# Places of 256 rows for the loaded rows of a routed expert layer, with small blocks loaded further ahead

## The chip, the cores and the metric

The kernel runs on one core of a Trainium2 chip. The metric is the device time of one execution in microseconds, the median of three runs. The engines are TensorE (PE, with its weight loads PEld), VectorE (DVE), ScalarE (ACT), GpSimd (POOL) and SyncE (SP). SP computes nothing here. It issues DMAs, one after another in the order of its queue, and a DMA that has to wait holds up every DMA behind it.

## The reference

A causal convolution of seven taps over 8 x 3584 tokens of 192 numbers (eight heads, each with its own taps), then a mixture of eight experts in which each token goes to one expert.

```python
w = softmax(weight)                                     # 8 heads x 7 taps
x = conv(x, w).reshape(28672, 192)                      # causal, per head
xn, en = x / (norm(x) + 1e-6), emb / (norm(emb) + 1e-6)
logits = xn @ en.T / tau
expert_idx = argmax(logits); gate_w = softmax(logits)[expert_idx]
for e in range(8):                                      # hidden width 1024
    mask = expert_idx == e
    out[mask] = gate_w[mask] * (relu(x[mask] @ w1[e]) @ w2[e])
```

## The kernel before

**Two streams.** The 28672 tokens come in 16 chunks of 1792 tokens (c0 to c15). A chunk is loaded (`load_x`, L355), convolved on PE (`mix`, L381), scaled and split into half-precision rows (`scaled`, `rest`), and turned by DMA transposes from SBUF to SBUF into `xtb` (`turn`, L619: four groups g of four transposes a chunk, all issued on SP). PE makes the logits from `xtb` (`logits`, L607), DVE ranks the tokens by expert (`rank`, L513, from the reduction at L518 to the row numbers `di` at L578), and POOL scatters the rows into the DRAM tensor `rows_d`, sorted by expert, in 16 indirect DMAs a chunk (`put` and `scatter`, L627). This is the dispatch stream.

The expert stream works off blocks of rows of one expert. `fetch` (L736) loads one block into SBUF: a register load, two DMA transposes from `rows_d` into the tile `e_xT` (L750) and one small DMA of token numbers and gates (L754), all on SP. `expert` (L772) makes the hidden layer, 40 matmuls into `h_ps` for a block of up to 256 rows and as many of 512 columns for one of 512 (L796), and then 24 matmuls into `o_ps` for each 128 rows (L819). Results are scaled by ACT (L824) and scattered to the output by POOL (L826).

**Blocks.** `hand_out` cuts blocks whenever enough chunks are ranked: b0 to b6 (256 rows) need the scatters of c0 and c1, b7 to b13 (256) those up to c2, b14 to b16 (512) and b17 to b24 (256) those up to c4, b25 to b31 (512) and b32 to b38 (256) those up to c7, b39 to b48 (512) those up to c11. The last 43, of 512, 256 and 128 rows mixed, need all (`last_blocks`). In all there are 37 loads of 256 rows, 34 of 512 and 21 of 128. `subs` holds the blocks in order, with the number of scatters that each needs. The index `at` is the block being worked on, `ready` the next to be loaded.

**What sets the order.** `run` (L930) interleaves the two streams by a plan of costs: after each step of a block it takes steps of the dispatch stream that are due, and one `put`. The order of SP's queue is that of the program (`manual_schedule`). On the other engines a scheduler orders the instructions when the kernel is built, by priority in the program and by what it thinks is ready; `behind` (L118) only keeps a convolution or logits matmul from going ahead of its planned place.

**Loading ahead.** `expert` calls `fetch` until the blocks up to `at + 2` are loaded. `e_xT` is a ring of three buffers of 512 rows, whatever the block's size, so a load waits until the block three before it has been through its `h_ps` matmuls. A load also waits for the scatters it needs. Two of the ring's buffers serve in the head of the kernel for other things: `head` (identity and ones for the norms of the weights, L173 and L315) and `cseq` (L225).

Of the kernel before, what the change touches and what calls it, by code (L numbers as in the profile page):

```python
# [12 lines left out]
F16 = mybir.dt.float16  # L13
F32 = mybir.dt.float32
# [8 lines left out]
H = 8  # L23
# [37 lines left out]
LEAD = 16.0  # L61
CAP = 6.0
MARGIN = 22
AHEAD_STEPS = 36


# [8 lines left out]
class _Moe:  # L75
    def __init__(self, ctx, tc, x, weight, emb, tau, w1, w2, out):
        self.tc, self.nc = tc, tc.nc
        self.x, self.weight, self.emb, self.tau = x, weight, emb, tau
        self.w1, self.w2, self.out = w1, w2, out
        B, S, _ = x.shape  # L80
        self.B, self.S, self.N = B, S, B * S
        self.nch = self.N // CT
        self.per_b = S // CT
        self.cap = self.N + PAD
        self.dummy = E * self.cap
        pool = lambda name, bufs, **k: ctx.enter_context(
            tc.tile_pool(name=name, bufs=bufs, **k))
        self.cp = pool("const", 1)
        self.xp = pool("xload", 2)
        self.sp = pool("small", 2)  # L90
        self.lp = pool("lone", 1)
        self.ep = pool("expert", 3)
        self.yp = pool("y", 3)
        self.op = pool("out", 4)
        self.mp = pool("meta", 6)
        self.rings = {k: pool("ps_" + k, n, space=PSUM)
                      for k, n in (("r", 2), ("l", 1), ("h", 5))}

        self.res = self.cp.tile([128, E * RES], F16, name="res")
        self.work = self.cp.tile([128, 2 * NFC * 512 + S2 + RES - W2], F16, name="work")  # L100
        self.hid = self.work[:, 0:2 * NFC * 512]
        self.slot = self.work[:, 2 * NFC * 512:]
        self.xtb = self.cp.tile([128, NT // GX, XW + HALO], F16, name="xtb")
        self.rows2 = self.cp.tile([TP, 2, NT, RW], I32, name="rows2")
        self.ids = self.cp.tile([TP, NT], I32, name="ids")
        self.xtn = 0
        self.wexp = self.cp.tile([128, E, 2], I32, name="wexp")
        self.dp = pool("scratch", 1, space=DRAM)
        self.rows_d = self.dp.tile([E * self.cap + PAD, RW], I32, name="rows_d")
        self.scatters, self.pend, self.step = [], [], None  # L110
        self.nput, self.final = 0, False
        self.counts, self.pace = {}, 1.0
        self.xts, self.mixed = [], {}
        self.subs, self.ready, self.at, self.copied = [], 0, 0, 0
        self.clock, self.mm = 0.0, None
# [51 lines left out]
    def constants(self):  # L167
        nc, cp = self.nc, self.cp
        nc.gpsimd.memset(self.xtb[:, :, XW:], 0.0)
        nc.gpsimd.memset(self.rows2[:, :, :, XD + 2:], 0)  # L170
        nc.gpsimd.iota(self.ids, pattern=[[TP, NT]], base=TP - 1,
                       channel_multiplier=-1)
        head = self.ep.tile([128, 4 * 512], F16, tag="xT", name="head")[:].bitcast(F32)  # L173
        self.idf, self.onef = head[:, 0:128], head[:, 128:256]
        make_identity(nc, self.idf)
        self.idh = cp.tile([128, 128], F16, name="idh")
        nc.vector.tensor_copy(out=self.idh, in_=self.idf)
        nc.gpsimd.memset(self.onef, 1.0)
        self.oneh = cp.tile([128, 128], F16, name="oneh")
        nc.gpsimd.memset(self.oneh, 1.0)  # L180

        self.lth = cp.tile([128, 128], F16, name="lth")
        nc.gpsimd.memset(self.lth, 1.0)
        nc.gpsimd.affine_select(
            out=self.lth, in_=self.lth, pattern=[[1, 128]], base=0,
            channel_multiplier=-1, compare_op=ALU.is_gt, fill=0.0)

        tmp = self.op.tile([128, D], F32, tag="y", name="tmp")[:, 0:2 * E + 64].bitcast(I32)
        e8i = tmp[0:TP, 0:E]
        nc.gpsimd.iota(e8i, pattern=[[-1, E]], base=E, channel_multiplier=0)  # L190
        self.e8 = cp.tile([TP, E], F32, name="e8")
        nc.vector.tensor_copy(out=self.e8, in_=e8i)

        self.rst = cp.tile([TP, E, NT], F32, name="rst")
        nc.gpsimd.memset(self.rst, 1.0)
        nc.gpsimd.memset(self.rst[:, :, 0:1], 0.0)

        nums = tmp[0:1, E:E + 64]
        nc.gpsimd.iota(nums, pattern=[[1, 64]], base=0, channel_multiplier=0)
        self.nums = cp.tile([1, 64], F32, name="nums")  # L200
        nc.vector.tensor_copy(out=self.nums, in_=nums)

        cbi = tmp[:, E + 64:]
        nc.gpsimd.iota(cbi, pattern=[[self.cap, E]], base=0, channel_multiplier=0)
        self.cb = cp.tile([128, E], F32, name="cb")
        nc.vector.tensor_copy(out=self.cb, in_=cbi)

        self.start = cp.tile([1, E], F32, name="start")
        nc.vector.tensor_copy(out=self.start, in_=cbi[0:1, :])

    def conv_taps(self, w):
        nc, cp = self.nc, self.cp
        m = cp.tile([H, 1], F32, name="cw_m")
        nc.vector.reduce_max(out=m, in_=w, axis=AX.X)
        nc.vector.tensor_scalar(out=w, in0=w, scalar1=m[:, 0:1], scalar2=None,
                                op0=ALU.subtract)
        z = cp.tile([H, 1], F32, name="cw_z")
        nc.scalar.activation(out=w, in_=w, func=AF.Exp)
        nc.vector.reduce_sum(out=z, in_=w, axis=AX.X)
        nc.vector.tensor_single_scalar(out=z, in_=z, scalar=1e-9, op=ALU.add)  # L220
        nc.vector.reciprocal(out=z, in_=z)
        nc.vector.tensor_scalar(out=w, in0=w, scalar1=z[:, 0:1], scalar2=None,
                                op0=ALU.mult)

        seq = self.ep.tile([128, 3 * 512], F16, tag="xT", name="cseq")[  # L225
            0:H, :].bitcast(F32)[:, 0:2 * 128]
        nc.vector.memset(seq, 0.0)
        nc.vector.tensor_copy(out=seq[:, TP + 9:TP + 9 + KT], in_=w)
        sd = self.dp.tile([H, 2 * 128], F32, name="cseq_d")
        nc.sync.dma_start(out=sd, in_=seq)  # L230
        self.more()
        self.band = cp.tile([128, H, TP], F32, name="band")
        run = sd[:, 0:TP]
        nc.sync.dma_start(out=self.band, in_=bass.AP(
            tensor=run.tensor, offset=run.offset,
            ap=[[1, 128], [2 * 128, H], [1, TP]]))
# [496 lines left out]
            out=self.slot[:, S2:], in_=self.res[:, bass.ds(self.we + W2, RES - W2)])  # L733


    def fetch(self):  # L736
        nc, tc = self.nc, self.tc
        sel, j, n, u, need = self.subs[self.ready]
        while len(self.scatters) < need:
            self.put()  # L740
        if u == 0:
            self.row = nc.sync.value_load(sel[0:1, j, 1:2], min_val=0,
                                          max_val=E * self.cap + PAD - n)
        row = self.row + u if u else self.row
        T = min(n, 512)
        nj = T // 128
        xT = self.ep.tile([128, 4 * 512], F16, tag="xT", name="e_xT")[
            :, 0:4 * T].rearrange("p (k t) -> p k t", t=T)
        src = self.rows_d[:].bitcast(F16)
        lds = [nc.sync.dma_start_transpose(  # L750
            out=xT[:, k:m], in_=src[bass.ds(row, T), o:o + 128 * (m - k)]).ins
            for k, m, o in ((0, 3, 0), (3, 4, 2 * D - 64))]
        mt = self.mp.tile([128, 4, 2], I32, tag="mt", name="e_mt")[:, 0:nj]
        lds.append(nc.sync.dma_start(  # L754
            out=mt, in_=self.rows_d[bass.ds(row, T), XD:XD + 2].rearrange(
                "(j p) c -> p j c", p=128)).ins)
        for i in lds:
            tc.declare_no_dep(i, group="put", keep=self.scatters[:need],
                              reason="loads name the scatters they need")
            tc.add_to_no_dep_group("get", i)  # L760
            for s in self.scatters[:need]:
                _dep(tc, i, s.name)
        self.subs[self.ready] = (sel, j, n, u, xT, mt, T)
        self.ready += 1
# [6 lines left out]

    def expert(self):  # L772
        nc, tc = self.nc, self.tc
        while self.ready < min(self.at + 3, len(self.subs)):
            self.fetch()
        sel, j, n, u, xT, mt, T = self.subs[self.at]
        self.copy_w1(self.at)
        if u == 0 and n >= 512:
# [116 lines left out]
    def steer(self, spent):  # L895
# [9 lines left out]
        self.rate = min(self.rate, 3.0)  # L905
        self.pace = (NT * self.end - self.nput) / max(1.0, steps - MARGIN)
        if self.final:
# [124 lines left out]
```

## Time and profile before

| | |
|---|---|
| time, median of 3 runs | 1249.96 us (1249.76 to 1250.8) |
| profiled execution, its own time | 1245.91 us |
| its span | 1244.2 us, mean granted TensorE clock 0.961 of full speed |
| PE busy | 1135.9 us, 91% of the span |
| DVE, ACT, POOL busy | 763.8, 592.5, 552.6 us |
| `h_ps` matmuls of small blocks (weights copied to `work`) | 2320, 232.4 us |
| loads of blocks | 184 transposes of `e_xT` in 92 loads |
| transposes of `xtb` by SP | 224 |

Times inside the execution are microseconds from the start of the span. A row of the engine timeline gives the start, the length, the engine, the line, the operation and how many were merged. Brackets at its end say how long the engine had been idle before it and what ended that. In the windows view PEclk is the granted clock of TensorE as a share of 2.4 GHz.

### The profile page before, as it was taken

The numbers are of one execution on the slowest core, as the hardware profiler recorded it, in microseconds if no ns is written. First come the engines' busy times: TensorE is split into PE (matmuls) and PEld (weight loads), VectorE is DVE, ScalarE is ACT, GpSimd is POOL, SyncE is SP. The second block draws the span as 40 slices with busy tenths as digits, with TensorE's granted clock in tenths as the row PEclk, the third lists the DMA queues.
The fourth block names the chain that finished last, engine by engine and source line by source line (L and its number), as shares of the span: only waits on it lengthen the run. The fifth ranks groups of instructions, "written<-read, shape, count | busy, mean of one in ns | idle before, by whom it ended". The sixth has DMA issues, their size and how long they took to land.

```text
span 1244.2 us, 31794 instructions
## 1 busy us (share of the span) xinstructions
PE 1135.9 (91%) x10620; PEld 881.2 (71%) x10620; DVE 763.8 (61%) x2042; ACT 592.5 (48%) x1359; POOL 552.6 (44%) x525
## 2 busy tenths in 40 slices
PE   4765869899999899998999999989999999999998
PEld 2543758776677876766887667757877786898797
DVE  3899667885766856666766474653335544465364
ACT  4986335455564464563546463333333434333333
POOL 0074166573565554646745456672222121222222
PEclk9676889999999999999999999999999999999999
DMA  9745576566666596654657645333222131223121
GB/s 255 216 146 147 120 162 147 119 168 145 135 157 165 97 185 146 131 140 97 165 105 170 115 94 125 87 96 66 65 45 61 41 75 43 43 54 72 42 52 28
DMA packets 305962, 140.69 MB, mean 113 GB/s; under 512 B 247774, under 2 KB 296285, under 8 KB 305808
## 3 DMA queue, kind: packets, MB, share of 16 engines
q1 hardware_dynamic: 282000, 87.97, 34.1%
q0 software_dynamic: 23808, 50.69, 14.7%
q8 instruction: 94, 1.54, 0.5%
q14 instruction: 60, 0.49, 0.1%
HBM read 38.35 MB, written 51.35 MB: 72 GB/s over the span
## 4 chain that ended last, share of the span: by engine, by line
issue 27%; PE 15%; POOL 8%; DMA 2%; ACT 1%; DVE 1%; POOLq 1%; ACTq 0%; DVEq 0%
POOL out_dram L826 7%; PE h_ps L796 7%; PE o_ps L819 6%; PE conv_ps L388 1%; DMA rows_d<-rows,di 1%; POOL rows_d L627 1%; DMA out_dram<-y,e_mt 1%; DMA xtb<-rows 0%; POOLq L826 0%; ACT work L800 0%; ACT sq L401 0%; PE lg_ps L611 0%; ACT rows L437 0%; DVE work L802 0%; DVE rows L444 0%
## 5 line engine op out<-in xcount | busy, mean ns | idle before, releaser
L819 PE MATMUL o_ps<-work 128*128 128x192 f16 x5544 | 503.2, 248 | 21.1 <-DVE work L802 9.2
L819 PEld LDWEIGHTS <-work 128*128 128x128 f16 x5544 | 462.5, 98 | 60.4 <-DVE work L802 15.7
L826 POOL DMA_INDIRECT out_dram<-y,e_mt x231 | 257.0, 1113 | 479.1 <-ACT y L824 439.2
L802 DVE SCALAR_TENSOR_TENSOR work<-h_ps,work 128x512 f16<-128x512 f32 x462 | 314.4, 685 | 175.2 <-ACT work L800 169.7
L800 ACT ACTIVATE work<-h_ps 128x512 f16<-128x512 f32 x462 | 271.3, 596 | 240.3 <-PE h_ps L796 206.1
L627 POOL DMA_INDIRECT rows_d<-rows,di x256 | 281.2, 1098 | 140.7 <-issue 57.1
L796 PE MATMUL h_ps<-e_xT,res 128*128 128x512 f16 x1360 | 311.2, 380 | 8.5 <-DVE work L802 5.9
L796 PEld LDWEIGHTS <-res 128*128 x1360 | 131.5, 98 | 162.7 <-issue 20.2
L796 PE MATMUL h_ps<-e_xT,work 128*128 128x256 f16 (+1 forms) x2320 | 232.4, 256 | 14.8 <-DMA e_xT<-rows_d 10.6
L796 PEld LDWEIGHTS <-work 128*128 128x128 f16 x2320 | 193.6, 99 | 40.7 <-DMA e_xT<-rows_d 9.9
L824 ACT ACTIVATE y<-o_ps,g 128x192 f32<-128x192 f32 x231 | 94.2, 419 | 235.6 <-PE o_ps L819 213.7
L732 DVE COPY work<-res 128x3074 f16 x88 | 85.3, 969 | 163.9 <-PE o_ps L819 163.8
L388 PE MATMUL conv_ps<-xt,band 128*112 128x384 f32 x256 | 112.5, 542 | 13.6 <-ACT xt L391 5.2
L437 ACT CAST rows<-xt 112x768 f16<-112x768 f32 x64 | 53.0, 832 | 97.4 <-DMA rows_d<-rows,di 49.2
L391 ACT COPY xt<-conv_ps 112x384 f32<-112x384 f32 x128 | 60.4, 480 | 43.0 <-PE conv_ps L388 41.5
L401 ACT ACTIVATE sq<-xt 112x192 bf16<-112x192 f32 x204 | 73.6, 361 | 4.8
L444 DVE TENSOR_TENSOR rows<-xt,rows 112x512 f16<-112x512 f32 x64 | 43.9, 685 | 45.7 <-ACT rows L437 35.3
L388 PEld LDWEIGHTS conv_ps<-xt,band 128*112 128x112 f32 x256 | 42.8, 194 | 32.0 <-issue 13.1
L435 DVE TENSOR_TENSOR xt<-xt,x_p_s 112x768 f32<-112x768 f32 x64 | 58.5, 950 | 0.0
L729 DVE COPY work<-res 128x3072 f16 x58 | 55.5, 957 | 0.3 <-PE h_ps L796 0.3
L611 PEld LDWEIGHTS <-xtb 128*128 128x128 f16 x768 | 30.1, 98 | 26.1 <-DMA xtb<-rows 12.9
L611 PE MATMUL lg_ps<-ma,xtb 128*128 128x16 f16 x512 | 30.6, 171 | 14.0 <-ACT xtb L502 7.1
(157 smaller groups left out, 520.5 us busy)
## 6 DMA issues: line engine op xcount, KB each, us to landing
xt<-in_dram SPq DMA_DIRECT2D x8, 1536.0 KB
xt<-in_dram SPq DMA_DIRECT2D x7, 1440.0 KB
rows_d<-rows,di POOLq DMA_INDIRECT x256
out_dram<-y,e_mt POOLq DMA_INDIRECT x231
xtb<-rows SPq DMA_TRANSPOSE x224
res<-in_dram SPq DMA_DIRECT2D x4, 768.0 KB
work<-in_dram SPq DMA_DIRECT2D x4, 768.0 KB
e_xT<-rows_d SPq DMA_TRANSPOSE x184
```

What stands on the lines that cost most here:

```text
L388: self.behind(nc.tensor.matmul(out=ps, lhsT=self.band[:, h, :], rhs=xt[:, :, h * G:(h + 1) * G], start=True, stop=True))
L391: nc.scalar.copy(out=xc[:, :, h * G:(h + 1) * G], in_=ps)
L401: nc.scalar.activation(out=sq, in_=xc[:, t, :], func=AF.Square, accum_out=n2[:, t:t + 1])
L611: i = self.nc.tensor.matmul(out=lg[:, g * GX + a, :], lhsT=xT[:, u:u + 128], rhs=self.mb if k == 2 else self.ma, start=(k == 0), stop=(k = ...
L627: i = self.nc.gpsimd.indirect_dma_start(out=self.rows_d[:, :], out_offset=bass.IndirectOffsetOnAxis(ap=idx, axis=0), in_=src, in_offset=No ...
L732: self.nc.vector.tensor_copy(out=self.slot[:, S2:], in_=self.res[:, bass.ds(self.we + W2, RES - W2)])
L796: mm = nc.tensor.matmul(out=ps[:, c, :], lhsT=w1(o, b + c), rhs=xT[:, k, :], start=(i == 0), stop=(i == 4))
L800: self.step = nc.scalar.activation(out=hh[:, b:b + m, :], in_=ps, func=AF.Relu).ins
L802: nc.vector.scalar_tensor_tensor(out=hl[:, b:b + m, :], in0=ps, scalar=0.0, in1=hh[:, b:b + m, :], op0=ALU.max, op1=ALU.subtract)
L819: mm = nc.tensor.matmul(out=o, lhsT=h[:, c, q], rhs=w2[:, c, k:k + D], start=(c + i == 0), stop=(c == NFC - 1 and i == 2))
L824: self.step = nc.scalar.activation(out=y, in_=o, func=AF.Copy, scale=g[:, a:a + 1]).ins
L826: i = nc.gpsimd.indirect_dma_start(out=self.out[:, :], out_offset=bass.IndirectOffsetOnAxis(ap=mt[:, a, 0:1], axis=0), in_=y, in_offset=No ...
```

## The change

The ring of three tiles becomes one tile `xr` of six places of 256 rows, the same memory. A block of up to 256 rows takes one place, one of 512 two neighbouring places that begin at an even one (`place`). `used` holds the last block in each place. `ahead` takes over from the loop in `expert`. Blocks up to `at + 2` are loaded as before. Beyond that a block is loaded as long as its places belong to blocks before `at` and its scatters have already been issued in the program. The head's helpers move into `xr`: `head` into places 0 and 1, `cseq` into place 2. The ring of the small tiles of token numbers goes from 6 to 10.

```diff
+HALF = 4 * 256
-        self.ep = pool("expert", 3)
-        self.mp = pool("meta", 6)
+        self.mp = pool("meta", 10)
+        self.xr = self.cp.tile([128, 6 * HALF], F16, name="xr")
+        self.turn_at, self.used = 0, [-1] * 6
-        head = self.ep.tile([128, 4 * 512], F16, tag="xT", name="head")[:].bitcast(F32)
+        head = self.xr[:, 0:2 * HALF].bitcast(F32)
-        seq = self.ep.tile([128, 3 * 512], F16, tag="xT", name="cseq")[
-            0:H, :].bitcast(F32)[:, 0:2 * 128]
+        seq = self.xr[0:H, 2 * HALF:].bitcast(F32)[:, 0:2 * 128]
+    def place(self):
+        w = 1 if self.subs[self.ready][2] <= 256 else 2
+        i = (self.turn_at + w - 1) // w * w % 6
+        return i, w
+
+    def ahead(self):
+        while self.ready < len(self.subs):
+            i, w = self.place()
+            near = self.ready < self.at + 3
+            if max(self.used[i:i + w]) >= self.at or not near and (
+                    self.subs[self.ready][4] > len(self.scatters)):
+                assert not near
+                return
+            self.fetch()
+
     def fetch(self):
         nc, tc = self.nc, self.tc
+        i, w = self.place()
+        self.turn_at = (i + w) % 6
+        self.used[i:i + w] = [self.ready] * w
...
-        xT = self.ep.tile([128, 4 * 512], F16, tag="xT", name="e_xT")[
-            :, 0:4 * T].rearrange("p (k t) -> p k t", t=T)
+        xT = self.xr[:, i * HALF:i * HALF + 4 * T].rearrange("p (k t) -> p k t", t=T)
...
     def expert(self):
         nc, tc = self.nc, self.tc
-        while self.ready < min(self.at + 3, len(self.subs)):
-            self.fetch()
+        self.ahead()
```

Worked through by hand from these rules and the order of the steps, the queue of SP reads as follows up to block 16. F3 is the load of b3, T3a and T3b are the two pairs of groups of transposes of chunk c3 (8 transposes each), X5 is the load of chunk c5, and a line is what stands between the starts of two blocks in the program.

```
        before                        after
start   F0 F1 F2 T2a X4 T2b           F0 F1 F2 T2a X4 T2b
b0                                    F3 F4 F5
b1      F3 T3a X5 T3b                 F6 T3a X5 T3b
b2      F4
b3      F5
b4      F6                            F7 F8 F9
b5      F7 T4a X6 T4b                 F10 T4a X6 T4b
b6      F8                            F11
b7      F9                            F12
b8      F10                           F13
b9      F11 T5a X7 T5b                T5a X7 T5b
b10     F12
b11     F13
b12     F14                           F14 F15
b13     F15 T6a                       T6a
b14     F16 X8 T6b                    F16 X8 T6b
b15     F17                           F17 F18
b16     F18 T7a X9 T7b                F19 F20 T7a X9 T7b
```

## Rows read from the trace of the kernel before

**Rows 1.** Busy time by stretch: PE, PEld, DVE, ACT, POOL, PEclk, DMA share, GB/s
```profile
290.00:850.00 560.00, 532.55 (x4723) 394.37 (x4722) 356.11 (x1067) 277.49 (x669) 322.17 (x302) 0.99 0.59 130
850.00:1100.00 250.00, 248.58 (x2384) 192.45 (x2383) 112.27 (x174) 95.22 (x179) 60.29 (x59) 1.00 0.25 53
```

**Rows 2.** Who waited for whom, PE, whole span: us in total, times, longest
```profile
PE lg_ps L611 <- DMA xtb<-rows: 11.8, 9, 3.6
...
PE h_ps L796 <- DMA e_xT<-rows_d: 10.6, 3, 6.0
```

**Rows 3.** Timeline of PE, 172 to 269 us: start, length, idle before and its end
```profile
172.92 0.21 PE L611 MATMUL lg_ps<-ma,xtb 128*128 128x16 f16 x2 [3.28 <-DMA xtb<-rows]
...
181.09 3.98 PE L796 MATMUL h_ps<-e_xT,work 128*128 128x256 f16 x22 [6.02 <-DMA e_xT<-rows_d]
184.90 0.20 PE L611 MATMUL lg_ps<-ma,xtb 128*128 128x16 f16 x2
...
227.19 1.27 PE L796 MATMUL h_ps<-e_xT,work 128*128 128x256 f16 x10 [3.66 <-DMA e_xT<-rows_d]
...
268.10 0.49 PE L796 MATMUL h_ps<-e_xT,work 128*128 128x256 f16 x3 [0.94 <-DMA e_xT<-rows_d]
```

**Rows 4.** Busy time by stretch around the two longest of these waits
```profile
174.00:184.00 10.00, 3.31 (x21) 2.31 (x21) 3.74 (x15) 1.99 (x3) 7.56 (x9) 0.50 0.75 142
...
228.00:232.00 4.00, 4.00 (x35) 3.01 (x32) 2.78 (x9) 1.19 (x2) 3.39 (x3) 0.57 0.54 119
```

**Rows 5.** Timeline of SP, 148 to 285 us: start, length of issuing, merged count
```profile
148.13 3.31 SPq L750 DMA_TRANSPOSE e_xT<-rows_d  x2
...
152.25 11.58 SPq L623 DMA_TRANSPOSE xtb<-rows  x8
...
164.54 12.34 SPq L623 DMA_TRANSPOSE xtb<-rows  x8
177.69 2.53 SPq L750 DMA_TRANSPOSE e_xT<-rows_d  x2
...
193.07 2.53 SPq L750 DMA_TRANSPOSE e_xT<-rows_d  x2
...
196.37 11.12 SPq L623 DMA_TRANSPOSE xtb<-rows  x8
...
208.67 13.37 SPq L623 DMA_TRANSPOSE xtb<-rows  x8
...
281.41 2.63 SPq L750 DMA_TRANSPOSE e_xT<-rows_d  x2
```

**Rows 6.** All loads of blocks: ns of one transpose, least/median/most, first and last start
```profile
L750 SPq DMA_TRANSPOSE e_xT<-rows_d x184: 1123/1232/2433, 111.1 to 1219.6; - x184
```

**Rows 7.** Timeline of PE, start of b14 (first matmuls with 512 columns)
```profile
289.50 0.81 PE L796 MATMUL h_ps<-e_xT,res 128*128 128x512 f16 x3
```

**Rows 8.** Timeline of DVE: first and last step of ranking chunks c3 and c4
```profile
185.91 0.41 DVE L518 TENSOR_REDUCE l<-lg_ps 112x128 f32<-112x256 f32 x1
...
201.92 0.17 DVE L578 TENSOR_SCALAR di<-dr 112x16 int32<-112x16 f32 x1
...
228.80 0.42 DVE L518 TENSOR_REDUCE l<-lg_ps 112x128 f32<-112x256 f32 x1
...
249.88 0.23 DVE L578 TENSOR_SCALAR di<-dr 112x16 int32<-112x16 f32 x1
```

**Rows 9.** Timeline of POOL: first and last of the 16 scatters of chunk c4
```profile
251.18 0.95 POOL L627 DMA_INDIRECT rows_d<-rows,di  x1 [0.30 <-DVE sl_ge L679]
...
278.20 1.24 POOL L627 DMA_INDIRECT rows_d<-rows,di  x1 [0.30 <-issue]
```

**Rows 10.** Timeline of PE: b0's matmuls and the first logits of chunk c2
```profile
116.84 4.53 PE L796 MATMUL h_ps<-e_xT,work 128*128 128x256 f16 x40
...
125.12 0.21 PE L611 MATMUL lg_ps<-ma,xtb 128*128 128x16 f16 x2 [3.59 <-DMA xtb<-rows]
```

**Rows 11.** Matmuls that read the head's ones: ns of one, first and last start
```profile
L315 PE MATMUL n_ps<-w_acc,head x16: 230/312/374, 22.6 to 104.1; 128*128 128x2 f32 x16
```

## The prediction

> **What bounds the kernel now.** I read the busy times by stretch first. From 290 us on PE is busy 532.6 of 560 us and then 248.6 of 250 us [rows 1], so whatever moves the time must either shorten PE's work, which this change does not touch, or take away idle time of PE before 290 us. The list of waits then says how much of that idle time is due to loaded rows: PE waited for `e_xT` three times, 10.6 us in all [rows 2]. The timeline shows all three: 6.02 us before b4, 3.66 us before b8 and 0.94 us before b12, and 3.28 us for transposes of chunk c3 just ahead of b4 [rows 3]. They add up to 13.9 us. Around them the granted clock is at its lower level of 1.2 GHz: 0.50 in the stretch 174 to 184, in which PE was busy 3.31 us, and 0.57 over 228 to 232 [rows 4]. At full clock that work would have taken 3.31 x 0.5 = 1.7 us and 4.00 x 0.43 = 1.7 us less. All that could be won is thus 13.9 + 3.4 = 17.3 us. The many small blocks after 850 us wait for no load at all (the three waits are the whole of it), so loading them earlier is worth nothing.
>
> Next is why these loads were late. SP's timeline shows the loads F4, F8 and F12 as the first behind the transposes of a chunk. For F4, a load takes its turn at 148.13 (F3), sixteen transposes and a load of x fill SP from 152.25 to 176.88, F4 starts at 177.69 [rows 5], and PE goes on at 181.09 [rows 3], 3.4 us after that start. SP, not the memory, was the queue that was full.
>
> **The change part by part.**
>
> *Number of instructions.* There are 92 loads before and after, with the same two transposes and one small DMA each, and the same 224 transposes of `xtb`. Nothing is added on any engine. What moves is the place of the loads in SP's queue. Blocks of 512 rows keep their distance of two.
>
> *Head.* `head` now lies in places 0 and 1, where F0 goes first, while before F0 had a free buffer. Its last reader starts at 104.1 [rows 11], and the first load at 111.1 [rows 6]. The wait is covered by 7 us. Without that cover it would be a delay of F0 by as much as the reader came later. The ring of 10 small tiles costs nothing in time, as nothing waits on it here.
>
> *Loads that move ahead of b4, b8 and b12.* F4, F5 and F6 now stand before T3a instead of behind T3b. F8, F9 and F10 stand before T4a, and F12 and F13 before T5a. The three waits for rows (10.6 us) and the clock's 3.4 us go.
>
> *What they are put in front of.* This is the other half. SP's queue is passed by three more loads before T3a and, in sum, three more before T4a (F0 to F10 instead of F0 to F7). One load takes 152.25 - 148.13 = 4.1 us of SP [rows 5]. So T3a and X5 start about 12.3 us later, at 164.6, and T3b ends at 189.2 instead of 176.9. F7 must wait for the scatters of c2 and cannot start before about 193.07, as now. Four loads follow, and T4a starts near 193.1 + 4 x 4.1 = 209.5 instead of 196.37: 13 us later. T4b ends at 208.67 + 13.37 + 13 = 235 instead of 222 [rows 5]. Before T5a the surplus is two loads, but one of those moves is already counted.
>
> What waits for T3 and T4: the logits on PE, the ranking on DVE, the scatters on POOL, and at last F14, the first load that needs c4. If PE meets the logits of c3 in the old place it idles (below). If it has b4 to b6 in SBUF it can do these first. Rows of the kernel before say that the order does give way: the logits of c2 are called before b0 in the program, and on PE the first of them stand behind all 40 `h_ps` matmuls of b0 and still wait 3.59 us for their transposes [rows 10]. I take it that this happens again, with new waits of 0 to 4 us at T3 and T4; 2 us.
>
> *The chain behind T4.* Now: T4b ends at 222, ranking runs from 228.80 to 249.88 (21.1 us) [rows 8], the scatters from 251.18 to 279.44 (28.3 us) [rows 9], F14 starts at 281.41 [rows 5], and b14 starts on PE at 289.50 [rows 7], 4.7 us after F14's data could be there (281.41 + 3.4). After: the logits of c4 can end about 1.3 us behind T4b, at 236.3. Ranking takes between 16.0 us (c3, 185.91 to 201.92) and 21.1 us (c4) [rows 8]. PE and DVE are then ahead of their plan, so the ranking's steps are the oldest work on DVE, and I take 16. The scatters take 28.3 us as now or, at the least, 16 times their spacing of 1.25 us = 20 us if POOL's scatters of results lie elsewhere (an estimate from lengths of 0.95 us and the 0.30 us before each [rows 9]); I take 25, nearer to the measured end. So 236.3 + 16 + 1.3 + 25 + 2 = 280.6 for F14, and 284.0 for its data. PE itself would be ready for b14 at 289.5 - 17.3 + 2 = 274.2. It therefore waits some 10 us there, in a new place, and comes back with the lower clock for a stretch (1.7 us, as after the wait at 181). b14's work then stands at 284.0 + 1.7 = 285.7, which is 3.8 us earlier than now. With the short ends (16, 20) F14's data is there at 279.0, a gain of 8.8; with the long ends (21.1, 28.3) at 292.4 and a loss of 4.6, each with the 1.7.
>
> *One rule against this.* Two transposes of a load take about 2.5 us of SP whether the block has 256 rows (177.69) or 512 (281.41) [rows 5], and the median of all 184, 128 rows among them, is 1.23 us each [rows 6]. The time is that of issuing. The Trainium skill, in DMA: Bandwidth & Descriptors, section Issuing engines are not separate DMA queues, says that the time a sequencer needs to initiate a DMA is usually small beside the DMA itself. By that, three more loads in front of T3 would hardly move it; the row says otherwise, since PE went on only 0.9 us after the issuing of F4 had ended.
>
> *After b14.* From there every load of the first 512 blocks waits as before, and later stages have no wait for rows to lose. What is won or lost at b14 stays to the end.
>
> **The rivals.**
>
> A. *The chain as long as now.* F14's data at 292.4 as worked out, b14 2.9 to 4.6 us late: the stall has only changed its place. For it: the scatters ran nearly back to back already [rows 9], and T4 had just 6 us to spare. Against it: PE's 17 us of freed time. The time is +3 us. It decides where ranking and scatters together take over 47 us.
>
> B. *PE's order stays as it is* (slower). Place: the logits of c3. T3b ends at 189.2, so the last group, which now starts at 184.90 [rows 3], starts at about 190, and PE idles at each group on the way. b4's wait is gone but PE is 5 us behind, with 1.7 us more at the lower clock. F14 comes no earlier than 284 there too, and the 3.66 us at b8 turn into a wait for T4b. The time is +6 us. It decides where the logits keep their place ahead of b4's matmuls.
>
> C. *SP is not held up.* If the transposes of T3 and T4 were as early as now, all of the 17.3 us less 2 would be won: -15 us. This is what the rule above gives. Against it stand the rows of issuing.
>
> D. *The change does not do what it says*: if the one tile `xr` were tracked as a whole, each block would wait for the load issued last, and behind every chunk's transposes (12 us and more a pair) PE would stand still. With some 10 us for each of the ten chunks from c3 to c12 that would be +100 us. Nothing in the trace speaks for it; the loads write separate column ranges.
>
> **How the numbers follow.** The profiled execution took 1245.91 us, 4.05 us under the median of 1249.96. Differences are carried over to the median. The forecast, -4 us, gives 1246.0, with its own range of 1240 to 1249; chance 0.46. A: 1253, chance 0.19. B: 1256, chance 0.18. C: 1235, chance 0.09. D: 1350, chance 0.02. The remaining 0.06 is for a new order on the engines that moves the time by 2 us either way. The range leaves out D, most of C and the far end of B: 1237 to 1256. A measurement of this kernel can tell about 0.2%, 2.5 us, from no change. The forecast case is faster by more than that in four of five outcomes, C always, so faster is 0.48. A is half within the bound, and with the rest of the forecast same is 0.24. B, half of A and D make slower 0.28.
>
> **What would show it.** In the profile after, PE should have no wait for `e_xT` before b4, b8 and b12. On SP three loads should stand one after another behind the transposes of c2, and T3a should start near 164.6, T4a near 209.5. A new wait of PE for `e_xT` should stand at b14, near 275 to 284, behind scatters that end near 279. If that wait is not there and b14 starts at 275, C was right. If PE waits for `xtb` some 10 us between 165 and 190, B was. If T4b does not end near 235, the price of a load on SP was wrong. The prediction fails altogether if blocks after 290 us change by more than a few us.

## The result and the profile after

The changed kernel takes 1257.61 us (median of 12 runs) where the kernel before takes 1250.38 (12 runs in the same rounds). The ratio is 1.0055, with a 95% interval of 1.0037 to 1.0074: slower, by some 7 us. The forecast was 1246.0 with a range of 1237 to 1256, so the time lies outside, 1.6 us above the upper end. The profiled execution of the changed kernel took 1255.78 us, its span is 1254.1 us. It lies 1.8 us under its median, that of the kernel before 4.5 us (1245.91 us), so the two profiles are 9.9 us apart where the medians are 7.2 us apart.

**SP's queue** does what the plan of the queue said. The timeline of SP (start, length of issuing, merged count), beside [rows 5]:

```profile
147.04 3.17 SPq L768 DMA_TRANSPOSE xr<-rows_d  x2
...
151.60 2.53 SPq L768 DMA_TRANSPOSE xr<-rows_d  x2
...
159.48 3.98 SPq L768 DMA_TRANSPOSE xr<-rows_d  x2
...
164.27 10.32 SPq L624 DMA_TRANSPOSE xtb<-rows  x8
...
175.31 12.68 SPq L624 DMA_TRANSPOSE xtb<-rows  x8
193.60 2.74 SPq L768 DMA_TRANSPOSE xr<-rows_d  x2
...
210.27 10.38 SPq L624 DMA_TRANSPOSE xtb<-rows  x8
...
221.85 12.36 SPq L624 DMA_TRANSPOSE xtb<-rows  x8
...
286.17 2.69 SPq L768 DMA_TRANSPOSE xr<-rows_d  x2
```

F4, F5 and F6 stand before T3a (164.27), F7 still starts at 193.60, behind the scatters of c2, and F8, F9 and F10 follow it before T4a (210.27). T4b ends at 234.2, 12.2 us later than before. F14 is the last row, at 286.17.

**PE's waits** before b14, 100 to 290 us (us in total, times, longest), first of the changed kernel, then of the kernel before in the same stretch:

```profile
PE lg_ps L612 <- DMA xtb<-rows: 20.4, 14, 4.1
```
```profile
PE h_ps L796 <- DMA e_xT<-rows_d: 10.6, 3, 6.0
PE lg_ps L611 <- DMA xtb<-rows: 10.2, 6, 3.6
```

The waits for loaded rows are gone, all three. In the same stretch the waits for transposes of `xtb` have doubled, from 10.2 to 20.4 us, so PE's waits of both kinds come to 20.4 us now and to 10.6 + 10.2 = 20.8 us before. The timeline of PE shows the longest of them, and two shorter ones at c4 and c5:

```profile
167.30 0.21 PE L612 MATMUL lg_ps<-ma,xtb 128*128 128x16 f16 x2 [3.12 <-DMA xtb<-rows]
185.08 0.21 PE L612 MATMUL lg_ps<-ma,xtb 128*128 128x16 f16 x2 [3.60 <-DMA xtb<-rows]
217.05 0.18 PE L612 MATMUL lg_ps<-mb,xtb 128*128 128x16 f16 x1 [0.91 <-DMA xtb<-rows]
230.29 0.22 PE L612 MATMUL lg_ps<-ma,xtb 128*128 128x16 f16 x2 [4.15 <-DMA xtb<-rows]
273.68 0.18 PE L612 MATMUL lg_ps<-mb,xtb 128*128 128x16 f16 x1 [0.97 <-DMA xtb<-rows]
```

b4 begins at 174.4 instead of 181.1 and b8 at 220.5 instead of 227.2, but b8 runs into the wait of 4.15 us, and b9 begins at 238.5 instead of 236.7. From there PE is behind: b14 starts at 293.63 instead of 289.50 [rows 7].

**The clock.** The windows view gives PE's busy time and the granted clock (PEclk, the number after POOL's). Three stretches that cover 160 to 290 us come first, and then all the stretches among them at the lower level of 1.2 GHz. After:

```profile
160.00:185.00 25.00, 17.39 (x179) 15.61 (x176) 17.74 (x63) 10.76 (x36) 19.23 (x15) 0.93 0.78 159
185.00:230.00 45.00, 39.25 (x386) 33.48 (x386) 32.84 (x90) 24.35 (x61) 28.88 (x26) 0.96 0.64 151
230.00:290.00 60.00, 53.71 (x526) 45.82 (x527) 42.93 (x152) 27.38 (x68) 32.92 (x29) 0.91 0.58 134
...
168.90:172.30 3.40, 3.40 (x26) 3.21 (x25) 2.85 (x7) 0.00 (x0) 3.40 (x1) 0.51 0.35 75
185.90:189.30 3.40, 3.40 (x29) 2.77 (x28) 2.84 (x11) 1.06 (x2) 2.49 (x4) 0.50 0.83 225
230.30:237.10 6.80, 5.82 (x52) 4.67 (x53) 3.14 (x7) 1.33 (x2) 3.90 (x4) 0.50 0.68 172
274.70:278.10 3.40, 3.34 (x20) 2.41 (x21) 3.13 (x9) 0.77 (x2) 2.79 (x3) 0.50 0.12 36
```

and the same of the kernel before:

```profile
160.00:185.00 25.00, 14.51 (x160) 12.54 (x159) 16.88 (x67) 10.05 (x34) 19.01 (x16) 0.80 0.78 174
185.00:230.00 45.00, 40.61 (x426) 35.06 (x424) 34.43 (x89) 25.08 (x63) 30.69 (x27) 0.98 0.64 152
230.00:290.00 60.00, 55.37 (x562) 47.92 (x561) 47.80 (x169) 29.15 (x72) 34.06 (x31) 0.99 0.61 140
...
173.70:183.90 10.20, 3.51 (x24) 2.43 (x25) 3.64 (x15) 1.99 (x3) 7.76 (x9) 0.50 0.72 144
228.40:231.80 3.40, 3.40 (x29) 2.46 (x27) 2.18 (x8) 1.19 (x2) 2.79 (x3) 0.50 0.63 138
```

From 160 to 290 us PE is busy 17.39 + 39.25 + 53.71 = 110.4 us after and 14.51 + 40.61 + 55.37 = 110.5 us before. It was busy as long and got less done, 1091 matmul records instead of 1148. At the lower clock it was, of this time, busy 3.40 + 3.40 + 5.82 + 3.34 = 16.0 us after, and 3.51 + 3.40 = 6.9 us before. Work at the lower clock takes about twice as long (14 `o_ps` matmuls take 2.40 us at 233.33 and 40 take 3.46 us at 265.47), so half of the difference, 4.5 us, is time lost. It is about what b14 is late (4.1 us). The long stretch of before (10.2 us at 0.50) cost little because PE stood idle for 6.7 us of it. The stretches of after fall on work. Not every wait is followed by such a stretch: from 160 us on there are 11 waits for transposes and four stretches.

**Behind b14** the busy times are near those of before: 290 to 850 us and 850 to 1100 us have PE busy 530.4 and 248.6 us, to be laid beside [rows 1]. Yet in this pair of executions another 5.8 us came between b14 and the last block (9.9 us later there, 4.1 at b14). The experiments say how far that belongs to the change.

### The profile page after: what moved, and what is told of

Its sections match the earlier page's. It is cut to its first block, busy times and chain, and to the rows that moved or that the text cites. A ratio compares the mean times of both kernels' runs of the same rounds, so it can differ in the third digit from the quotient of the medians.

```text
span 1254.1 us, 31838 instructions
## 1 busy us (share of the span) xinstructions
PE 1143.7 (91%) x10620; PEld 887.3 (71%) x10620; DVE 764.4 (61%) x2042; ACT 594.0 (47%) x1359; POOL 552.6 (44%) x525
## 4 chain that ended last, share of the span: by engine, by line
PE 43%; issue 3%; DMA 3%; ACT 2%; DVE 2%; POOL 1%; SPq 0%; POOLq 0%; ACTq 0%; DVEq 0%
PE h_ps L813 21%; PE o_ps L836 21%; PE conv_ps L389 1%; DMA rows_d<-rows,di 1%; ACT work L817 1%; POOL rows_d L628 1%; DVE work L819 1%; DMA out_dram<-y,e_mt 1%; DMA xtb<-rows 1%; DVE work L733 0%; DMA rows_d<-xtb,padi 0%; ACT rows L438 0%; ACT sq L402 0%; POOL out_dram L843 0%; SPq L768 0%
## 5 line engine op out<-in xcount | busy, mean ns | idle before, releaser
L836 PE MATMUL o_ps<-work 128*128 128x192 f16 x5544 | 510.3, 249 | 21.2 <-ACT work L817 7.9
L836 PEld LDWEIGHTS <-work 128*128 128x128 f16 x5544 | 467.4, 99 | 61.9 <-issue 15.8
L813 PE MATMUL h_ps<-xr,res 128*128 128x512 f16 x1360 | 311.6, 380 | 8.3 <-DVE work L819 3.9
L813 PEld LDWEIGHTS <-res 128*128 x1360 | 131.5, 98 | 162.8 <-issue 20.7
L813 PE MATMUL h_ps<-xr,work 128*128 128x256 f16 (+1 forms) x2320 | 232.4, 255 | 4.4 <-ACT y L841 2.6
L612 PEld LDWEIGHTS <-xtb 128*128 128x128 f16 x768 | 32.9, 99 | 40.2 <-DMA xtb<-rows 27.2
L612 PE MATMUL lg_ps<-ma,xtb 128*128 128x16 f16 x512 | 33.4, 171 | 21.0 <-DMA xtb<-rows 14.1
```

What stands on the lines that cost most here:

```text
L612: i = self.nc.tensor.matmul(out=lg[:, g * GX + a, :], lhsT=xT[:, u:u + 128], rhs=self.mb if k == 2 else self.ma, start=(k == 0), stop=(k = ...
L813: mm = nc.tensor.matmul(out=ps[:, c, :], lhsT=w1(o, b + c), rhs=xT[:, k, :], start=(i == 0), stop=(i == 4))
L836: mm = nc.tensor.matmul(out=o, lhsT=h[:, c, q], rhs=w2[:, c, k:k + D], start=(c + i == 0), stop=(c == NFC - 1 and i == 2))
```

## The experiments

All of these kernels have the six places. The theories go by letters that each quoted text explains for itself. On three of the chips that were used the kernel before takes 1339 to 1343 us (the last section shows one kernel, with the same instructions, on a chip of either kind). The interval there is about 0.3% to each side in the first runs, too wide to divide an effect of 0.5% into its parts, so three of the first four kernels were run once more on a chip where the kernel before takes 1250.78 us (35 runs). The fourth, `from_14`, was run on the slower chips alone.

### One part at a time

The condition for loading further ahead than two blocks is narrowed; `False` leaves the places alone.

```diff
-            if max(self.used[i:i + w]) >= self.at or not near and (
-                    self.subs[self.ready][4] > len(self.scatters)):
+            if max(self.used[i:i + w]) >= self.at or not near and (
+                    not (COND) or self.subs[self.ready][4] > len(self.scatters)):
# COND: places_only False; first_14 self.ready < 14; from_14 self.ready >= 14
```

The variant `before_last_group` loads two ahead, and one block more at a single point, ahead of the last group of four transposes of a chunk:

```diff
         for g in range(2, NT // GX):
+            if g == 3 and c > PICK[0]:
+                self.behind_turns(1)   # one fetch, if its place and scatters are there
             xTs.append(self.turn(c, g))
```

The first runs:

> The six places and the head's helpers in them stay, but no block beyond at + 2 is loaded, so the queue of SP has the order of the kernel before. Theory (loads in front of a chunk's transposes cost what they save): no difference, ratio 0.998 to 1.002, PE waits for loaded rows again before b4, b8 and b12 (some 10 us). Rival L (the layout itself costs, by the one tile, the head or another order on the engines): 1.004 to 1.007 as in the changed kernel. Rival S (the later stages lose, behind b14): no difference.

> Loading beyond at + 2 only for blocks b0 to b13, that is in front of the transposes of c3, c4 and c5. Theory: nearly all of the loss is here: ratio 1.003 to 1.006, b14 starts 4 us later than before, PE waits 18 to 22 us for transposed rows between 100 and 290 us and not at all for loaded rows. Rival L: 1.004 to 1.007. Rival S: 1.000 to 1.003, since half or more of the loss in the profile, 5.5 us, comes behind b14.

> Loading beyond at + 2 only from b14 on. Theory: 0.999 to 1.002; the transposes of c7 and later are finished 10 us or more before their logits, so a load or two in front of them costs nothing. Rival S: 1.003 to 1.005, with the additional time between b15 and b36. Rival L: 1.004 to 1.007.

> One load further ahead, and only between the third and the fourth group of a chunk's transposes (F4 in c3, F8 in c4, F12 in c5): 4.1 us of SP in front of one group instead of 12 in front of four. Theory: the waits for loaded rows fall from 10.6 to under 2 us, the fourth group of c3 lands 4 us later (near 182) and is wanted behind b4's first matmuls, so the new wait is 0 to 3 us; time 4 to 9 us less, ratio 0.993 to 0.997. Rivals L and S: no gain, 1.000 or more.

Measured, for places_only, first_14, from_14 and before_last_group as they stand above: 1.0032 (0.9998 to 1.0066), 1.0021 (0.9988 to 1.0055), 1.0027 (0.9993 to 1.006) and 0.9985 (0.9954 to 1.0015), beside 1343.47 us for the kernel before. All four intervals hold 1, and they tell nothing apart.

The second runs, on the chip with 1250.78 us, with the whole change once more:

> Places without loading further ahead, once more, since on the chip of the first call PE stood for over 60 us on issue, which the first trace of the kernel before does not show, and intervals were as wide as the effect. Theory: 0.998 to 1.002. Rival L (layout): the ratio of the changed kernel, 1.004 to 1.007.

> One load ahead, between the third and fourth group of a chunk's transposes, once more. Theory: 0.993 to 0.997; in the first call b4 started 6 us earlier than with the places alone (175.1 for 182.7) and the fourth group's logits still came 0.8 us earlier. Rivals: 1.000 or more.

> Loading further ahead for b0 to b13 alone, once more for the same reason. Theory: within 0.002 of the changed kernel's ratio. Rival S (later stages): 0.003 or more below it.

> The changed kernel itself, as the measure for the three beside it on the same chip. Both theories: ratio 1.004 to 1.007, waits of PE for transposed rows of some 20 us between 100 and 290 us, none for loaded rows.

| kernel | median us | ratio (95%) | T4b ends | F14 starts | b14 starts | last block starts | PE busy at 1.2 GHz | PE idle |
|---|---|---|---|---|---|---|---|---|
| places_only | 1248.21 | 0.9985 (0.9972 to 0.9998) | 222.6 | 281.4 | 289.5 | 1235.4 | 7.3 | 20.0 |
| before_last_group | 1249.36 | 0.9993 (0.9978 to 1.0009) | 229.2 | 284.6 | 292.7 | 1238.1 | 18.0 | 17.2 |
| first_14 | 1254.41 | 1.0028 (1.0012 to 1.0044) | 235.1 | 286.6 | 294.0 | 1243.0 | 15.8 | 20.2 |
| changed | 1256.21 | 1.0047 (1.003 to 1.0064) | 236.9 | 288.3 | 295.7 | 1242.3 | 17.2 | 20.7 |

The times of T4b, F14, b14 and the last block are from the timelines of SP and PE. The last two columns are from the windows view, in us from 160 us to the start of b14, with nearly the same number of matmul records in all four (1130 to 1135). PE's waits from 100 to 290 us in the same order, places_only first (two lines each for the first two kernels, one each for the others):

```profile
PE h_ps L813 <- DMA xr<-rows_d: 11.3, 3, 5.8
PE lg_ps L612 <- DMA xtb<-rows: 10.9, 7, 3.7
```
```profile
PE lg_ps L614 <- DMA xtb<-rows: 17.9, 13, 3.5
...
PE h_ps L825 <- DMA xr<-rows_d: 1.6, 2, 0.8
```
```profile
PE lg_ps L612 <- DMA xtb<-rows: 22.3, 14, 4.3
```
```profile
PE lg_ps L612 <- DMA xtb<-rows: 22.2, 15, 5.1
```

What follows. The six places and the head cost nothing (0.9985). Loading b0 to b13 further ahead costs what the change costs, or nearly: 1.0028 against 0.9985 is 0.43%, 5.4 us, and of these 4.5 us stand at b14 in the traces. The whole change is 6.2 us later than places_only at b14 and 6.9 us at the last block, so nearly nothing is lost behind b14 in this pair, and the 5.8 us that the first pair of profiles showed there are not seen again. `first_14`, which loads nothing further ahead behind b14, is 4.5 us late at b14 and 7.6 us at the last block, so some 3 us come and go there without such loads. Whether the loads after b14 cost anything stays open (1.0047 against 1.0028, and the intervals overlap).

The later T4b ends, the later F14 and b14 start, in all four kernels. But in none of them does PE wait for F14: b14 starts 7.4 to 8.1 us behind it, and where PE does wait for it (`late_logits`, below) b14 starts 4.1 us behind it. The sum of PE's two waits is 22.2, 19.5, 22.3 and 22.2 us: three of the four have the same, under other names. The kernel with the shortest waits, `before_last_group`, is no faster for it (0.9993), and the 0.993 to 0.997 expected of it did not come. The window of 230 to 290 us, places_only first, then `before_last_group`:

```profile
230.00:290.00 60.00, 55.63 (x566) 48.24 (x565) 48.81 (x172) 29.21 (x72) 32.84 (x30) 0.99 0.63 140
```
```profile
230.00:290.00 60.00, 56.18 (x540) 48.17 (x540) 46.03 (x159) 29.32 (x72) 30.51 (x27) 0.92 0.56 127
```

It is busier than places_only and has 540 matmul records where places_only has 566. The last two columns of the table do the sum for all of them. Against places_only, half of the additional busy time at 1.2 GHz plus the difference in idle time is 2.6, 4.5 and 5.7 us, and b14 starts 3.2, 4.5 and 6.2 us later. In `before_last_group` the idle time that went was paid back in clock.

### Logits taken later

If PE only waits because the logits of c3 to c5 are called too early for the later transposes, calling them later should give the gain.

```diff
-        yield self.clock + TURN
+        yield self.clock + TURN + (14.0 if 3 <= c <= 5 else 0.0)
```

> The changed kernel with the logits of c3, c4 and c5 planned 14 units later, so that on PE they stand behind more matmuls of blocks that are already loaded. Theory O (PE's order, built as if the transposes landed earlier, turns the delay into idle time): PE's waits for transposed rows fall from some 22 us to under 10, b14 starts 5 us or more earlier than in the changed kernel (before 290), ratio 0.996 to 1.001. Rival Q (SP's full queue and the chain from c4's transposes over ranking and scatters to the load of b14 set the pace): the waits fall as well, but b14 waits for its rows instead and starts at 292 to 297 as in the changed kernel; ratio 1.003 to 1.007.

Measured for this kernel, `late_logits`: 1401.39 us beside 1341.63, 1.043 (1.0378 to 1.0482), a loss far beyond both theories. PE's waits for transposes fell to 5.6 us, and PE reached b13 at 283.9 us, where another kernel on the same chip (first_7, below) reached it at 309.2. Then it stood still. Its timeline at b14, and SP's at F14:

```profile
322.65 3.62 PE L813 MATMUL h_ps<-xr,res 128*128 128x512 f16 x9 [27.55 <-DMA xr<-rows_d]
```
```profile
318.53 2.67 SPq L768 DMA_TRANSPOSE xr<-rows_d  x2
```

PE waited 27.55 us for the rows of b14, and 27.7 us more at b25. The ranking of c4 began at 276.0 there, 27 us behind the end of T4b, its last scatter ended at 316.7, and F14 followed 1.8 us later. So PE's early start is worth nothing beyond the point where the chain from the logits of c4 over ranking and scatters to F14 ends. That chain cannot begin before T4b is through, so loads ahead of T4 delay it too. Logits that come this late lose more than the waits cost; a shift of a few us, about as long as T4b is late, was not tried.

### The loads of b0 to b6 alone, and those from b14 on

With `self.ready < 7` three loads pass T3 but none more passes T4. This kernel, `first_7`, was run three times, and `from_14` once more. The texts are for `first_7`, `first_7`, `from_14` and `first_7`.

> Loading further ahead for b0 to b6 alone: three loads in front of c3's transposes, none in front of c4's, which start where they did before. Theory Q: b4 starts 4 to 6 us earlier, b8 still at 226 to 229, because its load ends there as before, and b14 within 1.5 us of the kernel with the places alone; ratio 0.997 to 1.001. Theory O: c3's waits alone cost 2 us or more at b14, 1.001 to 1.004.

> Six places; rows of the blocks b0 to b6 alone are loaded further ahead than two. Theory Q (the loss comes of the transposes of c3 and of c4 that stand behind loads, the last of them 12 us late, which feeds the chain ranking, scatters, F14, b14, and of waits spread over busy work at the lower clock): only T3 is passed by three more loads, T4 by the ones it has now, so F14 stays near 281 and the time is that of the places alone, 1247 to 1251 us (ratio 0.997 to 1.001), with b4 on PE at 174 to 178 and PE's waits for rows and for transposes between 100 and 290 us still 20 to 23 us in all. Theory O (any load in front of any chunk's transposes costs what it does): half of the loss of the loads of b0 to b13, 1252 us (1.0015).

> Six places; only blocks from b14 on are loaded further ahead than two. Theory Q: these blocks never waited for rows, and their loads pass nothing that PE waits for, so the time is that of the places alone, 0.9985 (0.997 to 1.000), b14 at 289 to 290 us. If the later loads cost by themselves what the changed kernel lost beyond the loads of b0 to b13: 1.0005 (0.9995 to 1.002), with b14 still at 289 to 290 and the difference standing behind it.

> Six places; rows of b0 to b6 alone are loaded further ahead than two. On a chip where the kernel before takes about 1250 us. Theory Q (what costs is T4 12 us later): T4a starts within 4 us of where it does before, b14 at 288 to 291 us, 0.997 to 1.001. Theory O (each load in front of transposes costs): 1.001 to 1.003, b14 at 291 to 292. On a chip where the kernel before takes about 1342 us: 0.998 to 1.003 either way, which tells nothing.

Measured: first_7 0.9996 (0.9969 to 1.0022), 1.0013 (0.9982 to 1.0044) and 1.0012 (0.9993 to 1.0031), from_14 1.0016 (0.9987 to 1.0046), all on chips where the kernel before takes 1339 to 1342 us. T4a starts at 201.0, 199.7 and 199.0 there, and at 202.0 in places_only on such a chip: T4 is indeed where it was. The times fit the theory that only the passing of T4 costs, but the other theory's 1.0015 lies in every interval. This stays undecided, as does the cost of the later loads.

### The transposes of c3 taken off SP

PE makes the transposes of c3 (48 small ones, and 12 copies on ACT), as it does for the first chunks in the head, so that the loads ahead of T3 pass nothing.

```diff
     def turn(self, c, g):
+        if c == 3:
+            return self.turn_pe(c, g)   # 12 PE transposes, 3 ACT copies
```

> Places without loading further ahead; the transposes of c3 are made by PE and copied by ACT, as those of c0 and c1 are, instead of by SP's DMAs: 24 us less in SP's queue between 150 and 180 us, some 5 us more on PE and 6 us more on ACT. Theory Q: the waits before b4 (5.8 us) and of c3's logits (4 us) go, F8 and c4's transposes come up to 20 us earlier as far as their rows are there, b14 starts 5 to 10 us earlier (280 to 285), ratio 0.990 to 0.995. Theory O: PE gains what it waited for rows, less its own 5 us: 0.996 to 1.000.

> The changed kernel with c3's transposes made by PE. Nothing is left that three early loads could hold up at c3, but F7 still waits for its scatters near 193 us and four loads stand in front of c4's transposes, so these start near 205 to 210 as in the changed kernel. Theory Q: better than the changed kernel (0.994 to 1.001) but behind the kernel with the places alone and c3 on PE, by 2 to 6 us. If loading ahead were good once SP has room: as good as that one or better.

> Six places, no load further ahead than two; the 16 transposes of chunk c3 are made by PE (48 small transposes) with ACT copying, so SP has 20 us less to issue ahead of F4. Theory Q (SP's queue is the bound before b14): F4 starts near 157 to 165 instead of 177.7, the wait of 6 us before b4 goes, PE gets about 4 us more work; T4 can start only as early as the rows of c4 are there. Time 1243 to 1250 (0.994 to 0.999). If SP isn't the bound there: no gain, 1250 to 1256, PE's new work being added (1.000 to 1.004).

> The changed kernel with the transposes of c3 made by PE and ACT, so that the loads that go ahead of T3 pass nothing. Theory Q: PE's waits between 100 and 290 us fall from 20 us to 12 or less, T4b ends 4 us or more earlier than 234, b14 at 288 to 291, time 1248 to 1253 (0.998 to 1.002), below the changed kernel's 1.0047 to 1.0055. If the loss is due to something other than the order on SP: 1.004 to 1.008.

> The changed kernel with c3's transposes made by PE and ACT. On a chip where the kernel before takes about 1250 us. Theory Q: PE's waits between 100 and 290 us fall from 20 us to 12 or less, T4b ends before 230, ratio 0.998 to 1.002, below the changed kernel's 1.0047 to 1.0055. If the loss is not due to the order on SP, or PE's and ACT's added work costs as much as it frees: 1.004 to 1.008. On a chip where the kernel before takes about 1342 us: 1.004 as twice before.

Measured, on two chips with 1339 to 1342 us for the kernel before: places with c3 on PE 1.0044 (1.0014 to 1.0073) and 1.0034 (1.0004 to 1.0063); the change with c3 on PE 1.0037 (1.0008 to 1.0065), 1.0042 (1.0009 to 1.0076) and 1.0037 (1.0009 to 1.0064). No gain came, in five runs. SP's timeline of the fourth of these shows why:

```profile
164.88 2.60 SPq L785 DMA_TRANSPOSE xr<-rows_d  x2
...
168.23 0.39 SPq L373 DMA_DIRECT2D xt<-in_dram  x1
198.52 2.59 SPq L785 DMA_TRANSPOSE xr<-rows_d  x2
...
214.86 1.20 SPq L641 DMA_TRANSPOSE xtb<-rows  x1
```

SP has nothing to issue for 30 us: F7 needs the scatters of c2, the last of which ends at 196.8, and starts at 198.52 whatever lies ahead of it, and T4a still stands behind F7 and the three loads that follow it. Freeing SP before F7 can't bring T4 forward. T4's delay comes from F8, F9 and F10 alone. The experiment took the wrong chunk. PE's waits for transposes up to 290 us did fall, to 1.6 to 2.1 us in the three runs of the change with c3 on PE, but b14 started at 317.4 to 323.8 us there and at 312.4 in places_only on such a chip. Whether the 0.4% is the price of the added work on PE and ACT is not shown, since the places alone had 1.0032 (0.9998 to 1.0066) on a chip of this kind.

## Why the prediction was wrong

*What bounds the kernel, and why the loads were late.* Right: SP's queue, and the three waits for rows went as said.

*What they are put in front of.* Right to within some 1 us: T3a 164.27 (said 164.6), T3b's end 188.0 (189.2), F7 193.60 (193.07), T4a 210.27 (209.5), T4b's end 234.2 (235). The price of a load on SP held, so rival C, in which SP is not held up, was wrong: the 12.2 us by which T4b is later are the issuing of three loads. The rule that stood beside C, from the Trainium skill, DMA: Bandwidth & Descriptors, section Issuing engines are not separate DMA queues, does not hold for the transposes on this queue, where one load takes some 4 us of SP [rows 5].

*What waits for T3 and T4: the step that failed.* The prediction let the order on PE give way, with new waits of 0 to 4 us and 2 us taken. The new waits are 20.4 - 10.2 = 10.2 us, as much as the waits for rows that went (10.6). At T3 they grew by 3.2 us, at T4 by 6.9 us, from none. So the 17.3 us that the prediction took off PE's way to b14, less 2, did not come off. The order did give way, but for the last groups only: in PE's order the four groups of logits of c3 stand behind 304, 348, 352 and 374 expert matmuls before, and behind 304, 347, 420 and 447 after; those of c4 behind 656, 700, 704, 714 and 656, 702, 740, 746. The first two groups of each did not move, the last moved by 73 and by 32 matmuls. That is 8.3 and 3.6 us at the rate of [rows 10] (40 in 4.53 us), against transposes that come 12 us later. The rows from which the prediction took its rule, the logits of c2 behind b0 [rows 10], showed a group that gives way and still waits 3.59 us; the prediction named that wait and yet took 2 us for both chunks together.

*The clock: a second term of the wrong sign.* The prediction took 3.4 us away with the waits and put 1.7 us back. Measured, the loss at the lower clock rose by 4.5 us. It had read the stretch of 10 us at 0.50 [rows 4] as a cost of the wait, rightly, at 1.7 us; but it did not see that about the same waiting in more and shorter pieces (14 waits instead of 9) could bring more such stretches, and over busy work. By the sums above that is where b14's delay comes from: PE's idle time is unchanged.

*The chain behind T4: sized too short.* Its rows after:

```profile
236.20 0.42 DVE L519 TENSOR_REDUCE l<-lg_ps 112x128 f32<-112x256 f32 x1 [2.07 <-PE lg_ps L612]
...
253.58 0.17 DVE L579 TENSOR_SCALAR di<-dr 112x16 int32<-112x16 f32 x1
```
```profile
254.03 0.95 POOL L628 DMA_INDIRECT rows_d<-rows,di  x1 [1.90 <-DVE sl_av L670]
...
282.34 0.95 POOL L628 DMA_INDIRECT rows_d<-rows,di  x1 [0.30 <-issue]
```

The start was right, 236.20 (said 236.3). Ranking took 17.4 us (16) and the scatters 29.3 (25): POOL's other scatters lay among them as before [rows 9], and the hoped-for shortening to 25 had only an estimate behind it. With F14 at 286.17 and 3.4 us for its data, the chain allowed b14 at 289.6, where it stood before (at 290.3 with the 4.1 us that the rows of `late_logits` show for this block of 512 rows). So by the chain alone the change would have won nothing at b14, rival A's case with a price near zero. What made it a loss was PE, which came to b14 only at 293.63, 3 to 4 us later than the data.

*The rivals.* B came nearest, with +6 us and the price at T3 and T4; its sign, some 10 us of waits for `xtb` between 165 and 190, was 3.12 + 0.97 + 3.60 = 7.7 us there, and the wait of 4.15 us with smaller ones followed at T4. Its condition, logits that keep their place, held for half of the groups. It was given 0.18, less than the forecast's 0.46, on the strength of one row. The upper end of the range, 1256, was B's own point, with nothing above it for B coming out dearer.

*Head, ring, later blocks.* Right: the places alone cost nothing, and PE's busy time from 850 to 1100 us is unchanged. The prediction's own sign of failure, more than a few us behind 290 us, stood in the first pair (5.8 us) and not in the second (0.7 us), so it decides nothing.

What is shown: the loss goes with the loads of b0 to b13 (`first_14` against `places_only`), the waits of the changed kernel have another name and nearly the same sum, and b14 cannot start before the chain from c4's logits is through (`late_logits`), though in the change PE comes later still. That the lower clock over busy work makes up most of the 3 to 6 us at b14 is added up from the traces, over nearly the same work and, but for `before_last_group`, nearly the same idle time; it was not tried by itself, since no kernel here kept the waits and changed the clock. Why the clock fell in one place and not in another, and whether the loads ahead of T3 cost anything without those ahead of T4, stays open.

## What to carry to other kernels

When one queue issues both the work that is late and the work that feeds the next stage, putting one in front of the other may only change which wait PE meets, as it did here; ask of every step that is passed who waits for it next, and look whether the waits add up to less. The same waiting can also cost more in several pieces than in one: here, from 160 to 290 us, 15.1 us in 6 waits for loads and transposes went with 6.9 us of work at the lower clock, and 16.0 us in 11 waits with 16.0 us. A first step that lets an order "give way" wants a count of the instructions by which it can, held against the time by which the input is later.

## What was not expected of the hardware

*Two levels of time for one program.* places_only on two chips, with the same 31876 instructions, has spans of 1333.1 and 1245.4 us. Its waits that the profile puts down to nothing but "issue", over the whole span, and the windows of 850 to 1100 us; first on the chip with 1343 us for the kernel before, then on the other:

```profile
PE o_ps L836 <- issue: 45.5, 56, 2.8
PE h_ps L813 <- issue: 11.8, 16, 2.5
...
850.00:1100.00 250.00, 227.71 (x2025) 167.50 (x2024) 108.98 (x246) 83.71 (x159) 80.03 (x79) 0.95 0.27 61
```
```profile
PE h_ps L813 <- issue: 1.9, 2, 1.3
PE o_ps L836 <- issue: 0.4, 1, 0.4
...
850.00:1100.00 250.00, 248.58 (x2369) 191.78 (x2366) 112.39 (x174) 95.31 (x179) 59.03 (x59) 1.00 0.26 55
```

In these two groups PE idles 57.3 us on the first chip for no wait that the profile shows, and 2.3 us on the second, and the clock is down with it. What holds PE up there is not shown by any row.

*How little can stand ahead of a lower clock.* In the changed kernel two waits of 0.97 and 0.53 us, which ended at 273.68 and 274.44, were all that stood close ahead of the stretch at 274.70 to 278.10, in which PE was busy 3.34 of 3.40 us at 0.50. A short wait need not bring it: the kernel before waited 0.94 us ahead of b12 [rows 3] and has no such stretch near it.
